# A two-branch kernel on one core: early products padded with zeros, loads and tables regrouped, and a new order of work

## The chip, the core and the metric

The kernel runs on one core of a Trainium2 chip. A core has a matrix engine (TensorE, PE in the profile; its weight loads are PEld), a vector engine (VectorE, DVE), a scalar engine (ScalarE, ACT), GpSimd (POOL) and SyncE (SP), which here only issues DMA transfers. Each engine works through its own queue in order and waits on semaphores for the others. The metric is the device time of one execution in microseconds; the kernel before has a median of 127.74 us over three runs (127.66 to 128.27).

## What is computed

Two independent branches whose outputs are put side by side, for 2048 tokens and width D = 448:

```python
# A: attention with 16 heads of 28, each token sees 8 tokens at distances 0, 2, ..., 14
qkv = x @ wqkv
logits = q . k[pos - off] * scale ; masked where pos - off < 0
attn = softmax(logits) ; o = attn . v ; a = o @ wo
# B: a diagonal complex state space of 448 states
Lam_bar = exp(exp(log_dt) * Lam) ; B_bar = (Lam_bar - 1) / Lam * Bmat
h[t] = Lam_bar * h[t-1] + B_bar x[t]
b = 2 * Re(C h) + x * Dskip
out = concatenate([a, b])
```

## The kernel before

All 2048 tokens are held in SBUF. The tokens of A are loaded in three parts: the first 512, the second 512 and the last 1024 (u = 0 is the first 1024, u = 1 the last). The first 1024 are transposed on TensorE (XI for the first 512, XA and XH for the second 512) and copied from PSUM into xT (xi, xa, xh); the last 1024 are transposed by DMA (L176). D = 448 is split into three blocks of 128 and one of 64: the block of 64 is kept for both halves s of 512 tokens at once, half 0 on partitions 0 to 63 and half 1 on partitions 64 to 127.

Queries and keys are made in seven column groups m (even m queries, odd m keys, m = 6 the rest of both, packed by wj): QK(u, m, k) is a step for both halves s. With k = 0 it runs the three blocks of 128 rows for both halves, with k = 1 the two products of 64 rows, one per half, on the two halves of the array. QS(m, s) (L349) is the same for one half, used at the start: three products of 128 rows (L354) and one of 64 (L355). Results go from PSUM to SBUF by qk and qh. V_ and v make the values in the same way.

P(u, r, ws) multiplies queries with four shifted views of the keys on VectorE (L385, 2048 wide) into one of seven buffers pr; E_(u, r) sums them per head with narrow products on TensorE (32 columns of the array; E_06 and E_16 also with 64 rows). lt, TD, sma, smb and smc make the softmax. AL, al, ad and sp lay the weights out as bands in the tile PT through DRAM; AV multiplies them with the values (32 columns of the array again), W_ with wo.

For B, PP transposes the raw parameters, and pcopy, pa, pb, pc, pd_, pe, pf and pg make the constants from them: pa is the exponential of log_dt on ScalarE, pc five further exponentials rk, pf sines, pg sixteen small operations on VectorE. The states stand in seven groups g of 64 complex ones. ty and tf make the angles of a group (ScalarE and VectorE, 256 wide), ts(0..2, g) the sine, the absolute value and the cosine on ScalarE. BD transposes B by DMA into BT, xt transposes the tokens of B into xbuf, where the tokens of A stood. BU multiplies the two (again k = 0 whole, k = 1 the halves of 64 rows). BR, z, UP and y carry four tokens together, sa, sb and sd are the scan of a pair of groups on VectorE, DN, dn, H_, h, hp, hy and hz bring the states back to all tokens, and C, c and oc give the output.

The order of all this is written out by hand in ORDER (L32). Each word is one step; the digits are its arguments, the digits after @ the PSUM banks it takes, and a final point or an equals sign puts a copy on ScalarE or on VectorE. Instructions enter each engine's queue in that order, and an engine never runs a later instruction before an earlier one. The loads at the start are issued by SP, the small parameters and one weight piece by ScalarE; a transfer waits for the one eight places before it.

Of the kernel before, what the change touches and what calls it, by code (L numbers as in the profile page):

```python
# [9 lines left out]
BF16 = mybir.dt.bfloat16  # L10
# [9 lines left out]
N2 = NC // 2  # L20
# [12 lines left out]
WU@0 XI0@1 xi00. xi01. XI1@2 XI2@3 xi10= xi11. PP@4 xi20= pcopy pa QS00@5 pb QS10@6 qk000. pd_ pc XH1@7 pe XA10@0 xh1=  # L33
XA11@1 qk010. xa10= QK021@32 xa11. QK031@45 P000 ty0 QS01@6 pf QS11@7 P001 QK051@01 QK030 tf0 qk011. qk001. pg ty5 tf5
ts00 ts10 qk030. ts20 QK020 qk020. ts05 QK041@76 P010 ty2 tf2 BD QK050 qk031. QK040 wj= QK061@43 ts15 qk050. ts02
qk051. qk021. P011 P020 P021 qk041. V_111@50 ts25 QK060 P030 ty1 qk040. V_000@12 E_00@67 E_01 qh001. P031 tf1 qh000.
P040 qh011. qh010. V_110 V_001 v000. ts12 P041 hc0 E_03 P050 P051 P060 v001. v110. E_02 V_010@43 v111. V_011 ts01 ts11
v010. ts22 ty6 tf6 QK110@12 QK111 QK100@50 QK101 P061 qk110. QK121@41 qk100. E_05 E_04 qk101. P100 P101 qk111. v011.
QK130@50 E_06 QK131 ts21 ty4 tf4 qk131. QK120 qk130. lt00 lt01 qk120. qk121. ts06 ts16 ts26 E_10@23 P110 QK150@30
QK151 ts04 ts14 qk151. QK141@56 QK161@74 P111 QK160 qh110. P120 P121 P130 ts24 qk150. QK140 qk141. qh111. V_100@10  # L40
V_101 v100. qk140. v101. P131 TD0 sma0 xt1 qh101. V_500@36 V_501 P140 v500. V_411@41 xt0 E_12 xt2 hc1 xt3 V_410 qh100.
LC V_400@50 V_401 v501. v410. v400. E_11 v411. E_13 V_510@76 smb0 P141 P150 P151 v401. E_14 V_511 ty3 P160 E_15
BU001@45 v511. BU101@10 P161 E_16 lt11 lt10 TD1 BU100 smc0 OZ v510. z10. BU200@63 BU000 LD ab ci2= CD2 ci0. CD0 rb0
ci3. CD3 z00. AL0@2 al0. ci1= AL1@7 al1. BR11 z11. BR01 BU010@14 z01. CD1 sma1 smb1 BU201 z20. tf3 BU011 BU301@27 BR02
BU111@05 z02. BU300 ts03 dk= BR03 rb3 smc1 BR21 ad1 z21. z30. z03. BU211@61 BU110 BR12 BU210 z12= BR13 BR22 BU401@32
xd0 ca3 ca6 ad0 cs3 z22. UP0 BR31 y0= xd3 xd1 OP pm3 BU400 wo AX@0 cs6 z13. z31. UP1 y1. ax. z40. sa0 ca1 BU310@46
BU500@75 BU501 BU311 z50= pm4 BR41 BR32 AL2@0 ca2 al2. z32. sb0 BU511@37 z41. BR23 z23= pm0 BR51 pm1 z51. sp0 AL3@0
BU510 BR33 ts13 al3. z33. BR52 BU411@42 z52. cs1 sp1 UP3 y3. UP2 y2. sd0 BU601@50 cs2 ts23 sa2 DN0@3 BR53 z53. BU410
ca4 BR42 DN1@6 dn1 BU600 z42. hp021 BR43 sb2 z60. dn0 UP5 AV020@1 AV031@6 sd2 AV000@4 z43. av031. cs4 UP4 y4. BU611@35
y5. av020. AV010@6 adx av010. AV030@2 AV021@7 BR61 BU610 sa4 z61. DN3@1 ad2 dn3 sb4 BR62 av021. AV001@6 av000. av030.  # L50
AV011@0 H_03@7 DN2@4 z62. BR63 dn2 ad3 H_00@2 W_20@1 z63= UP6 av011. H_01@3 h03 av001. W_01@0 ca5 ca0 W_11@6 w20= sd4
pm2 w01. w11. hp012 sp2 spx y6= h00 sa6 W_21@4 sp3 H_02@7 W_10@1 ow20 cs0 DN4@0 W_00@6 hp020 w10. w00. w21. W_31@5 h02
hp011 W_30@2 w30. sb6 DN5@1 AV111@6 AV110@4 av111. dn5 dn4 AV100@7 ow01 AV120@2 w31. av120. av110. ow11 AV121@1
AV131@6 cs5 sw2 ow10 av121. hp013 AV130@0 hp025 sw0 AV101@5 hp112 hp014 sd6 av100= C32@2 sw4 h01 hp023 DN6@4 dn6
av131= hp122 hp016 av130. hp022 hp120 hp010 C30@1 hp111 av101= H_05@7 h05 hp121 H_04@3 H_06@4 h04 h06 C33@6 C31@5
hp123 W_71@7 hp110 c30 oc30 xd2 hp113 sw6 ow30 ow31 hp125 hp115 c31 c32 oc32 c33 hy2 hy1 C00@3 W_60@4 c00 hz2 hy0 w71.
hz1 W_51@0 W_50@1 hp114 hy3 hp015 hz0 C02@5 C01@2 hz3 hp124 hp024 hp126 W_61@6 w61. hp026 hy5 hy4 oc31 ow71 ow00 C03@3
ow21 oc33 c01 oc01 hz5 hp116 W_40@7 hz4 hy6 W_41@6 w51. w50. W_70@2 ow51 hz6 C12@0 ow61 w41. w60. C11@1 c02 c03 C10@6
c10 c11 c12 w40. w70. C13@4 ow60 C20@5 C21@7 ow50 oc00 ow40 C22@3 CH0@2 c13 oc02 ow41 oc10 oc11 oc03 oc12 ow70 CH1@6
oc13 c20 c21 oc21 c22 oc20 oc22 ch0 oh0 ch1 oh1  # L60
# [3 lines left out]
def kernel(  # L64
# [109 lines left out]
    xT = s2.tile([128, 2, 7, 512], BF16, tag="xT")  # L174
# [15 lines left out]
    hpib, phi, sg, sscale = (cols[:, i:i + 1] for i in range(4))  # L190
    POOL.memset(hpib, 0.5 * PI * SHR)
    for col, lo, hi in ((phi, 0.0, 0.25), (sg, 2.0, -2.0), (sscale, 2 * PI * SHR, -2 * PI * SHR)):
        POOL.memset(col[0:64], lo)
        POOL.memset(col[64:128], hi)
# [85 lines left out]
    @op  # L280
    def XI(h):

        p = pp["xi", h] = ps(BF16)
        if h == 2:
            for t in range(4):
                PE.transpose(p[0:64, 128 * t:128 * t + 128], xnA[:, t, 384:448], ident[:])
            return
        for t in range(2):
            for f in range(3):
                PE.transpose(p[:, 256 * f + 128 * t:256 * f + 128 * t + 128], xnA[:, 2 * h + t, 128 * f:128 * f + 128], ident[:])  # L290

    @op
    def xi(h, k, e):
        p, c = pp["xi", h], 256 * h
        if h == 2:
            evict(e, xT[0:64, 0, 3], p[0:64, 0:512])
# [20 lines left out]
    @op  # L317
    def XH(b):
        p = pp["xh", b] = ps(BF16)
        for t in range(4):  # L320
            PE.transpose(p[64 * b:64 * b + 64, 128 * t:128 * t + 128], xnA[:, 4 * b + t, 384:448], ident[:])

    @op
    def xh(b, e):
        r = slice(64 * b, 64 * b + 64)
        evict(e, xT[r, 0, 3], pp.pop(("xh", b))[r, 0:512])
# [6 lines left out]
    def wqk(m, rows, kt):  # L333

        if m < 6:
# [13 lines left out]
    def QS(m, s):  # L349
# [5 lines left out]
        PE.matmul(p[:], wqk(m, slice(64 * s, 64 * s + 64), 3), xT[64 * s:64 * s + 64, 0, 3], start=False, stop=True)  # L355
# [243 lines left out]
    def pd_():  # L599
# [3 lines left out]
        V.tensor_scalar(fT[:], fT[:], -1.0, None, ALU.mult)  # L603
# [41 lines left out]

    @op
    def ty(g):
        pp["fr", g] = keep.tile([128, N2], F32, tag="fr", name="fr", bufs=2)
        ACT.activation(pp["fr", g][:], iot[:], ACTF.Identity, scale=fT[:, g:g + 1])

    @op
    def tf(g):

        kM, fr = keep.tile([128, N2], F32, tag="kM", name="kM")[:], pp["fr", g][:]
# [4 lines left out]
    def ts(i, g):  # L659

        fr = pp["fr", g][:]
        if i == 0:
            ACT.activation(tab[:, 1, g], fr, ACTF.Sin, scale=sscale)  # L663
        elif i == 1:
            ACT.activation(fr, fr, ACTF.Abs)
        else:
            ACT.activation(tab[:, 0, g], fr, ACTF.Sin, bias=hpib, scale=-2 * PI * SHR)
# [8 lines left out]
    @op  # L676
    def BD():
        SP.dma_start(BT.rearrange("p g b n -> p (g b) n"), Bn.rearrange("p g d -> p (g d)"), transpose=True)
# [305 lines left out]
```

## Time and profile before

| | |
|---|---|
| median of three runs | 127.74 us |
| the profiled execution, whole | 128.18 us |
| its span, first to last instruction | 126.5 us |
| mean granted TensorE clock | 1.000 |
| products on TensorE | 1045 |
| DMA | 22.33 MB in 57604 packets |

The page of the profile gives the busy time of each engine, the chain of work that ended last, and the costliest groups of instructions; further views give the timeline (start, duration, engine, line, operation, shapes, and in brackets the idle time just before and what ended it), the groups by line with the mean duration in ns, and the busy time of each engine in chosen stretches. In such a stretch the columns are the length, then PE, PEld, DVE, ACT and POOL busy with their instructions, the granted clock, the DMA share and GB/s. A merged row of the timeline, such as x3, runs from the first start to the last end. The numbers by which the change is judged are shown with the prediction.

### The profile page before, as it was taken

Reading aid. Unit: us, or ns where it says so; the run is one execution under the profiler, and the core shown is the slowest. Engines: PE = TensorE matmul, PEld = TensorE weight load, DVE = VectorE, ACT = ScalarE, POOL = GpSimd, SP = SyncE. Lnnn points to the kernel's source line nnn. Section 1 sums busy time; section 2 is a strip of 40 time slices with the busy share of each in tenths; the row PEclk is TensorE's granted clock in tenths of the full one; section 3 lists DMA queues with packets and bytes.
Section 4 is the critical chain, followed back from the end, with each engine's and each line's share of the span. In section 5 each row is a group of like instructions: output and inputs, shape, how many; then the busy total and the mean of one; then the engine's idle time right before and its main releaser. Section 6 shows DMA issues by size and latency. Waiting matters only on the chain.

```text
span 126.5 us, 2882 instructions
## 1 busy us (share of the span) xinstructions
PE 119.8 (95%) x1045; PEld 56.8 (45%) x1053; DVE 113.9 (90%) x220; ACT 105.2 (83%) x209; POOL 21.8 (17%) x40
## 2 busy tenths in 40 slices
PE   6989999999999999999999999999999999999990
PEld 6542334333334343463334444644585555555560
DVE  5769899999999999999999999999999999993850
ACT  0859999998899989898999999999999999991000
POOL 6800000000000002960199920000000000000000
PEclk9999999999999999999999999999999999999999
DMA  3896998999999998269899899899964242436442
GB/s 98 233 227 166 277 293 160 155 225 208 194 249 212 211 213 209 77 134 166 269 297 154 138 141 353 209 115 145 140 174 110 48 136 86 149 110 218 153 145 66
DMA packets 57604, 22.33 MB, mean 177 GB/s; under 512 B 44183, under 2 KB 57047, under 8 KB 57591
## 3 DMA queue, kind: packets, MB, share of 16 engines
q1 hardware_dynamic: 57384, 22.12, 79.7%
q8 instruction: 8, 0.13, 0.5%
q10 hardware_dynamic: 207, 0.04, 0.2%
q14 instruction: 5, 0.04, 0.1%
HBM read 9.86 MB, written 6.37 MB: 128 GB/s over the span
## 4 chain that ended last, share of the span: by engine, by line
DVE 40%; PE 33%; ACT 13%; DMA 6%; issue 4%; DVEq 0%; ACTq 0%
DVE pr L385 19%; PE ps L865 16%; PE ps L553 9%; DMA xbuf<-in_A_x_dram 4%; ACT Z L114 3%; ACT ctmp L690 2%; DVE fr L656 2%; PE ps L540 2%; DMA raw<-in_B_Lambda_re_dram 2%; DVE R L672 2%; DVE z L444 2%; PE ps L795 1%; PE ps L246 1%; ACT qf L114 1%; ACT kf L114 1%
## 5 line engine op out<-in xcount | busy, mean ns | idle before, releaser
L385 DVE TENSOR_TENSOR pr<-qf,kf 128x2048 bf16<-128x2048 bf16 x24 | 27.8, 1219 | 0.0
L246 PE MATMUL ps<-xbuf,BT 128*128 128x512 bf16 (+1 forms) x108 | 24.0, 380 | 0.5 <-issue 0.3
L865 PE MATMUL ps<-Cw,Z 128*128 128x448 bf16 x105 | 21.0, 353 | 0.0
L246 PE MATMUL ps<-xT,wq 128*128 128x512 bf16 (+1 forms) x94 | 20.5, 381 | 0.4 <-issue 0.2
L246 PEld LDWEIGHTS <-BT 128*128 128x128 bf16 (+1 forms) x112 | 9.0, 97 | 12.3 <-issue 3.7
L865 PEld LDWEIGHTS <-Z 128*128 128x128 bf16 x105 | 10.2, 98 | 9.5
L114 ACT CAST Z<-ps 128x512 bf16<-128x512 f32 (+1 forms) x29 | 13.7, 524 | 0.4 <-PE ps L741 0.2
L553 PE MATMUL ps<-wo,oT 128*128 128x448 bf16 x64 | 13.4, 352 | 0.0
L246 PEld LDWEIGHTS <-wq 128*128 128x128 bf16 (+1 forms) x96 | 7.2, 97 | 12.4 <-issue 4.7
L246 PE MATMUL ps<-wq,xT 128*128 128x448 bf16 (+1 forms) x64 | 12.6, 355 | 0.0
L941 POOL MEMSET PT<- 128x4320 f32 x3 | 11.0, 3696 | 5.5 <-ACT tab L663 5.5
L690 ACT ACTIVATE ctmp<-Cw,c2t 64x448 f32<-64x448 bf16 x14 | 9.3, 666 | 0.2
L553 PEld LDWEIGHTS <-oT 128*128 128x128 bf16 x64 | 6.2, 98 | 5.8
L114 ACT CAST v_s<-ps 128x448 bf16<-128x448 f32 x16 | 8.1, 531 | 0.5 <-PE ps L246 0.4
L246 PEld LDWEIGHTS <-xT 128*128 128x128 bf16 (+1 forms) x64 | 5.0, 97 | 7.8 <-issue 3.8
L114 ACT CAST ya<-ps 128x448 bf16<-128x448 f32 (+1 forms) x16 | 7.9, 548 | 0.6 <-DMA out_dram<-ya 0.6
L114 ACT CAST oT<-ps 128x512 bf16<-128x512 f32 x14 | 7.8, 628 | 0.1
L114 ACT CAST qf<-ps 128x512 bf16<-128x512 f32 x12 | 6.8, 595 | 1.4 <-PE ps L355 0.9
L917 POOL MEMSET Z<- 128x14 bf16 x1 | 0.1, 113 | 43.5 <-DMA Cr<-in_B_C_re_dram 43.5
L114 ACT CAST kf<-ps 128x512 bf16<-128x512 f32 x12 | 6.8, 576 | 0.5 <-PE ps L246 0.5
L729 PE MATMUL ps<-Z,R 128*128 128x512 bf16 x20 | 6.6, 381 | 0.2 <-DVE Z L114 0.2
L397 PE MATMUL ps<-pr,E 128*32 128x512 bf16 x96 | 6.7, 383 | 0.0
(168 smaller groups left out, 214.2 us busy)
## 6 DMA issues: line engine op xcount, KB each, us to landing
PT<-pd SPq DMA_DIRECT2D x16, 156.0 KB, 4.5
out_dram<-ya SPq DMA_DIRECT2D x16, 112.0 KB, 1.7
out_dram<-xbuf SPq DMA_DIRECT2D x15, 112.0 KB, 1.7
pd<-Ak SPq DMA_DIRECT2D x2, 640.0 KB, 3.3
xbuf<-in_A_x_dram SPq DMA_DIRECT2D x2, 448.0 KB
xnB<-in_B_x_dram SPq DMA_DIRECT2D x4, 224.0 KB
xnB<-in_B_x_dram SPq DMA_DIRECT2D x4, 192.0 KB, 4.6
PT<-Z SPq DMA_DIRECT2D x6, 128.0 KB, 3.5
```

Of the source, the lines that this page charges most:

```text
L114: (ACT.copy if e == "A" else V.tensor_copy)(o, i)
L246: PE.matmul(o, l, r, start=(first and i == 0), stop=(not first and i == len(pairs) - 1 and not more[s]))
L385: V.tensor_tensor(t[:], q.unsqueeze(1).to_broadcast((128, 4, 512)), k4, ALU.mult)
L397: PE.matmul(acc[s][32 * i:32 * i + 32], E[:, f, ws, :], t[:, i, :], start=(f == 0 and ws == 0), stop=False)
L444: V.reciprocal(z[:, :, 16:32], z[:, :, 0:16])
L540: PE.matmul(p[32 * hh:32 * hh + 32, 128 * bl:128 * bl + n], v_s[:, t, 4 * hg + hh, :], PT[:, t % NS, (4 * hg + hh) // HS, (4 * hg + hh) % ...
L553: PE.matmul(p[:, 0:D], late["oT"][:, b // 4, hg, par, 128 * (b % 4):128 * (b % 4) + 128], late["wo"][:, hg, :], start=(hg == 0), stop=(hg ...
L656: V.scalar_tensor_tensor(fr, kM, MAGIC, fr, ALU.subtract, ALU.subtract)
L690: ACT.activation(t[a:a + 64, 0:D], Cw[b:b + 64, g, :], ACTF.Copy, scale=c2t[a:a + 64, g:g + 1])
L729: PE.matmul(pp["z", g, j][:], rot(g, 0), late["Z"][:, g, j - 1, :], start=False, stop=True)
L865: PE.matmul(p[:, 0:D], z, Cw[:, g, :], start=(g == 0), stop=(g == G - 1))
L941: POOL.memset(late["PT"][:, 4 * i:4 * i + 4].rearrange("p t g n -> p (t g n)").bitcast(F32), 0.0)
```

## The change

Six things change at once.

1. The last products of QS become 128 rows high. A new tile wzz holds the 64 weight rows of half 0 with zeros under them, and those of half 1 with zeros above them; a memset puts zeros into the half of xT that is not yet filled. Three memsets on VectorE stand ahead of the ones for v_s and Ak. All eight QS (m = 0 to 3, s = 0 and 1) are used, where before m = 2 and 3 went through QK.
2. The transposes of the last 64 columns (XI2, XH) take 128 columns, of which the copy reads the upper half.
3. The weight columns 128 to 255 are loaded ahead of the second 512 tokens, and the first half's small piece is one transfer of 256 columns from ScalarE's queue instead of two of 128.
4. The sign of the sine for the lower 64 partitions goes into the angle (way instead of sscale), and the three steps ts run over two groups at once, 512 wide (the seventh group alone): 12 activations instead of 21.
5. The DMA transpose of B is issued in two parts, four groups and three.
6. ORDER is written anew, with other banks and other engines for some copies. xi00, xi01, two more al, three more w and three more y are on VectorE; xi10, the first xa, wj, dk, one more av and two more z on ScalarE.

```diff
 ORDER = """
-WU@0 XI0@1 xi00. xi01. XI1@2 XI2@3 xi10= xi11. PP@4 xi20= pcopy pa QS00@5 pb QS10@6 qk000. pd_ pc XH1@7 pe XA10@0 xh1=
-XA11@1 qk010. xa10= QK021@32 xa11. QK031@45 P000 ty0 QS01@6 pf QS11@7 P001 QK051@01 QK030 tf0 qk011. qk001. pg ty5 tf5
+WU@0 XI0@1 xi00= xi01= XI2@2 PP@3 pcopy pa XI1@4 xi10. xi20= pb pd_ pc pe xi11. QS00@5 QS10@6 QS30@7 XH1@0 ty0 ty1 pf
+tf0 tf1 XA10@1 xh1= QS20@3 pg ab rb0 ts00 xa10. XA11@2 xa11. QK050@40 qk000. xt0 qk010. P000 qk020. QS11@1 qk011. P001
+QS01@2 qk001. qk030. ts10 P010 ts20 ty4 QS21@5 QS31@6 qk031. qk021. QK041@31 tf4 QK051 P011 V_101@27 QK040 V_100 wj.
...
+    wzz = s2.tile([128, 2, 2, 256], BF16, tag="wzz")
+    for r in range(2):
+        V.memset(wzz[64 * r:64 * r + 64, 1 - r].rearrange("p a n -> p (a n)").bitcast(F32), 0.0)
+    xT = s2.tile([128, 2, 7, 512], BF16, tag="xT")
+    V.memset(xT[64:128, 0, 3], 0.0)
...
+        if c < 256 and len(at) == 2:
+            o = wzz[64 * s:64 * s + 64, s, :, c:c + n]
         eng.dma_start(o, i)
...
-    w_half(0, 0, 128, 0, D, eng=ACT)
+    w_half(0, 0, 256, 0, D, eng=ACT)
     SP.dma_start(xnA[:, 0:2], xA_r[:, 0:2])
     SP.dma_start(xnA[:, 2:4], xA_r[:, 2:4])
     w_load(0, 128, 0, D)
+    w_load(128, 128, 0, D)
     SP.dma_start(xnA[:, 4:8], xA_r[:, 4:8])
     w_half(1, 0, 256, 0, D)
-    w_load(128, 128, 0, D)
-    w_half(0, 128, 128, 0, D)
...
-            PE.transpose(p[64 * b:64 * b + 64, 128 * t:128 * t + 128], xnA[:, 4 * b + t, 384:448], ident[:])
+            PE.transpose(p[:, 128 * t:128 * t + 128], xnA[:, 4 * b + t, 320:448], ident[:])
...
-        PE.matmul(p[:], wqk(m, slice(64 * s, 64 * s + 64), 3), xT[64 * s:64 * s + 64, 0, 3], start=False, stop=True)
+        PE.matmul(p[:], wzz[:, s, m % 2, 64 * (m - m % 2):64 * (m - m % 2) + 128], xT[:, 0, 3], start=False, stop=True)
...
-        V.tensor_scalar(fT[:], fT[:], -1.0, None, ALU.mult)
+        V.tensor_scalar(fT[:], fT[:], way, None, ALU.mult)
...
-    def ts(i, g):
-
-        fr = pp["fr", g][:]
+    def ts(i, q):
+
+        fr, gs = pair(q, pp["fr", q]), slice(2 * q, 2 * q + 2 if q < 3 else G)
         if i == 0:
-            ACT.activation(tab[:, 1, g], fr, ACTF.Sin, scale=sscale)
+            ACT.activation(tab[:, 1, gs], fr, ACTF.Sin, scale=2 * PI * SHR)
...
-    def BD():
-        SP.dma_start(BT.rearrange("p g b n -> p (g b) n"), Bn.rearrange("p g d -> p (g d)"), transpose=True)
+    def BD(i):
+        gs = slice(4 * i, 4 + 3 * i)
+        SP.dma_start(BT[:, gs].rearrange("p g b n -> p (g b) n"), Bn[:, gs].rearrange("p g d -> p (g d)"), transpose=True)
```

In the rest of the new order, up to the first product of B (BU300, before it was BU001), the steps on which the timing of the start depends follow each other like this: QK060, V_000, V_011, QK061, V_001, E_00, E_02, E_01, V_010, V_400, QK110, E_03, QK100, QK120, E_04, E_05, E_06, lt00, lt01 on TensorE and ScalarE; on SP xt0, TD0, BD0, xt2, xt3, xt1, the loads of C, BD1, TD1. The first band product is AV021 (before AV020), and the last scan is followed by C32 and DN6 in both.

More of the change, by code (lines that the diff above doesn't have):

```diff
@@ L43 @@
[L43 to L47, printed above, removed]
@@ L189 @@
     cols = const.tile([128, 5], F32, tag="cols")
-    hpib, phi, sg, sscale = (cols[:, i:i + 1] for i in range(4))
+    hpib, phi, sg, way = (cols[:, i:i + 1] for i in range(4))
     POOL.memset(hpib, 0.5 * PI * SHR)
-    for col, lo, hi in ((phi, 0.0, 0.25), (sg, 2.0, -2.0), (sscale, 2 * PI * SHR, -2 * PI * SHR)):
+    for col, lo, hi in ((phi, 0.0, 0.25), (sg, 2.0, -2.0), (way, -1.0, 1.0)):
         POOL.memset(col[0:64], lo)
@@ L285, in XI @@
             for t in range(4):
-                PE.transpose(p[0:64, 128 * t:128 * t + 128], xnA[:, t, 384:448], ident[:])
+                PE.transpose(p[:, 128 * t:128 * t + 128], xnA[:, t, 320:448], ident[:])
             return
@@ L333, in wqk @@
     def wqk(m, rows, kt):
+        if m < 4 and kt == 3:
+            return wzz[rows, rows.start // 64, m % 2, 64 * (m - m % 2):64 * (m - m % 2) + 128]
         if m < 6:
@@ L644, with pair @@
     tab = keep.tile([128, 2, G, N2], BF16, tag="tab")
+    def pair(q, t):
+        return t[:, 0:2 if q < 3 else 1]
     @op
     def ty(g):
-        pp["fr", g] = keep.tile([128, N2], F32, tag="fr", name="fr", bufs=2)
-        ACT.activation(pp["fr", g][:], iot[:], ACTF.Identity, scale=fT[:, g:g + 1])
+        if ("fr", g // 2) not in pp:
+            pp["fr", g // 2] = keep.tile([128, 2, N2], F32, tag="fr", name="fr")
+        ACT.activation(pp["fr", g // 2][:, g % 2], iot[:], ACTF.Identity, scale=fT[:, g:g + 1])
     @op
     def tf(g):
-        kM, fr = keep.tile([128, N2], F32, tag="kM", name="kM")[:], pp["fr", g][:]
+        kM, fr = keep.tile([128, N2], F32, tag="kM", name="kM")[:], pp["fr", g // 2][:, g % 2]
         V.tensor_scalar(kM, iot[:], fT[:, g:g + 1], MAGIC, ALU.mult, ALU.add)
@@ L666, in ts @@
         else:
-            ACT.activation(tab[:, 0, g], fr, ACTF.Sin, bias=hpib, scale=-2 * PI * SHR)
+            ACT.activation(tab[:, 0, gs], fr, ACTF.Sin, bias=hpib, scale=-2 * PI * SHR)
     @op
```

52 lines of the change are left out of this document (27 added, 25 removed).

## The prediction

> **What bounds the kernel now.** I read the page first (busy shares, chain of waits), then the busy time by stretch, then TensorE's part of the timeline from 5 to 13 us.
>
> ```profile
> span 126.5 us, 2882 instructions
> PE 119.8 (95%) x1045; PEld 56.8 (45%) x1053; DVE 113.9 (90%) x220; ACT 105.2 (83%) x209; POOL 21.8 (17%) x40
> ...
> DVE 40%; PE 33%; ACT 13%; DMA 6%; issue 4%; DVEq 0%; ACTq 0%
> ```
> ```profile
> 13.00:95.00 82.00, 80.83 (x812) 35.78 (x818) 79.93 (x145) 78.14 (x157) 16.91 (x11) 1.00 0.97 197
> 95.00:123.10 28.10, 28.03 (x155) 14.94 (x153) 23.94 (x51) 19.15 (x35) 0.00 (x0) 1.00 0.43 128
> ```
>
> From 13 to 95 us TensorE is idle for 82.00 - 80.83 = 1.17 us, VectorE for 2.1, ScalarE for 3.9; from 95 to 123.1 us only TensorE is full. The chain runs through VectorE and ScalarE because they are full too, but the end is TensorE's queue run dry. So a change pays if TensorE has less to do or waits less, and if the other two keep up. The granted clock is 1.00 throughout.
>
> "Busy" hides one thing, which shows in single starts:
>
> ```profile
> 6.75 0.82 PE L354 MATMUL ps<-xT,wq 128*128 128x512 bf16 x3
> 7.50 0.39 PE L355 MATMUL ps<-xT,wq 64*128 64x512 bf16 x1
> 8.39 0.41 PE L321 MATMUL ps<-ident,xbuf 128*64 128x128 bf16 x4 [0.50 <-DMA xbuf<-in_A_x_dram]
> 8.73 0.84 PE L307 MATMUL ps<-ident,xbuf 128*128 128x128 bf16 x12
> 9.64 0.60 PE L246 MATMUL ps<-xT,wq 64*128 64x512 bf16 x4
> 10.18 0.82 PE L354 MATMUL ps<-xT,wq 128*128 128x512 bf16 x2
> 10.93 0.39 PE L355 MATMUL ps<-xT,wq 64*128 64x512 bf16 x1
> 11.25 0.82 PE L354 MATMUL ps<-xT,wq 128*128 128x512 bf16 x3
> ...
> 12.54 2.27 PEld L246 LDWEIGHTS <-wq 128*128 128x128 bf16 x12 [0.42 <-issue]
> ```
>
> Three whole products of 512 columns last 0.82 and one lasts 0.39, so a start follows a start after (0.82 - 0.39)/2 = 0.215: a slot. From the half product at 10.93 to the next whole one at 11.25 it is 0.32; from 6.75 to the half product at 7.50 it is 0.75, not 0.645. Every change of the tile's shape, in or out, costs 0.10 to 0.11 us in which nothing runs.
>
> **The change part by part.** *Shapes.* Shapes are 128x128, half rows (64x128), 32 columns (E_, AV), E_06 and E_16 (64x32), 64-column transposes, and PP (7 rows). Going through both order lists, the shape changes 76 times before, 56 after. The eight half products of QS and the 64-column transposes become whole, and the later halves of QK, V_ and BU stand next to each other more often. At 0.10: -2.0 us (-1.6 to -2.2).
>
> *Padded halves.* For m = 0 to 3 of the first 1024 tokens there were 4 x 4 slots (QS) and, for m = 2 and 3, 12 whole products and 4 halves that run two at a time: 30 slots. Now 8 x 4 = 32: +0.43 us. TensorE's own sum: -1.5 us. [...]
>
> *The way to 13 us.* The new order puts new work in front of the first products, so I walk it with these rows (the first is the chain of waits).
>
> ```profile
> 2.91 5.44 DMA xbuf<-in_A_x_dram
> ```
> ```profile
> 1.05 0.48 DVE L227 MEMSET v_s<- 128x512 uint32 x1
> 2.02 2.19 DVE L229 MEMSET Ak<- 128x2560 f32 x1 [0.48 <-issue]
> 4.13 0.13 DVE L233 TENSOR_TENSOR Is<-ident 128x64 bf16<-128x64 bf16 x1
> ...
> 4.83 0.76 DVE L114 COPY xT<-ps 128x512 bf16<-128x512 bf16 x2 [0.58 <-PE ps L290]
> 5.52 0.16 DVE L582 CAST P<-ps 128x21 f32<-128x21 bf16 x1
> 5.71 0.21 ACT L586 ACTIVATE dt<-P 128x7 f32<-128x7 f32 x1
> 5.96 0.43 DVE L590 TENSOR_TENSOR are<-dt,P 128x7 f32<-128x7 f32 x1 [0.28 <-ACT dt L586]
> ...
> 7.33 0.60 ACT L596 ACTIVATE rk<-are 128x7 f32<-128x7 f32 x5
> ...
> 9.62 0.58 ACT L114 COPY xT<-ps 128x512 bf16<-128x512 bf16 x1 [1.10 <-PE ps L307]
> 10.00 2.35 DVE L385 TENSOR_TENSOR pr<-qf,kf 128x2048 bf16<-128x2048 bf16 x2
> 10.10 0.51 ACT L649 ACTIVATE fr<-iot,fT 128x256 f32<-128x256 f32 x1
> 10.62 1.28 ACT L615 ACT_TABLE_LOAD   x1
> ...
> 12.54 0.56 ACT L114 CAST kf<-ps 128x512 bf16<-128x512 f32 x1
> 13.00 0.59 ACT L114 CAST qf<-ps 128x512 bf16<-128x512 f32 x1
> ```
> ```profile
> L663 ACT ACTIVATE tab<-fr,cols 128x256 bf16<-128x256 f32 x7 | 3.6, 513 | 0.1
> ...
> L114 ACT COPY xT<-ps 128x256 bf16<-128x256 bf16 x2 | 0.7, 376 | 0.0
> ```
>
> Three memsets of 256 words are new on VectorE: v_s and Ak give (2.19 - 0.48)/2048 = 0.83 ns a word, so 0.27 each, 0.8 together, of which 0.48 may fall into the hole before Ak. Is then ends at 4.6 to 5.1. Three copies follow (0.34, 0.22, 0.16): the constants are out at 5.3 to 5.8. On ScalarE the exponential (0.21) now stands ahead of xi10 (0.58): 6.1 to 6.6. Then rk (0.60), released by VectorE's "are" after xi20, and xi11 (0.38) behind it: 7.1 to 7.6. That is what QS00's third product waits for. Two slots, then QS10 and QS30 with four each: 9.2 to 9.7.
>
> There XH1 needs the second 512 tokens, which landed at 2.91 + 5.44 = 8.35. Now two weight loads go out ahead of them; bounds are 8.35 (the loads run beside them anyway) and 10.6 (issued 1.3 later, and 192 KB at the 226 GB/s of the row below). I take 9.3, the issue alone: no wait.
>
> ```profile
> 5.00:10.00 5.00, 4.11 (x34) 1.79 (x31) 3.78 (x18) 2.92 (x12) 1.30 (x4) 1.00 0.91 226
> ```
>
> ScalarE meanwhile has two ramps (0.41 apart), the table load (1.28), three small ones (0.64) and the first sine of two groups. A copy of 512 takes 0.21 more than one of 256, so that sine takes 0.51 + 0.21 = 0.72: 10.5 to 11.1. Behind it stand xa10 (1024 wide, 0.58 + 0.42 = 1.0), xa11, and two evictions at 0.46: xa10 is there at 11.5 to 12.1, VectorE's first product P000 starts at 13.0 to 13.5, not at 10.00. TensorE waits for xa10 before QK050's second product and ends QK050 at 12.7 to 13.3; I take 13.0.
>
> At 13.0 the old kernel has run 16 slots of QS, 2 pairs at 9.64, one pair at 12, and 2 of the products begun at 12.54: 21. The new one has 22, of a total that is 2 larger, so one slot more is left (+0.2), but 54 shape changes against 62 (-0.8). From 13 us on TensorE has 0.6 us less: **-0.6** (-0.9 to -0.3 by the dates; +0.7 with the tokens at 10.6).
>
> *VectorE.* By 13 us it has done the pg block, two tf and rb0, which came later before: some 4.6 us more ahead of P000, while up to the last scan it gets 1.8 more (al, y and w evictions come over, xa10, wj and two z leave). So 2.8 less is left, and P000 is 3.0 to 3.5 later: 0.2 to 0.7 late at the last scan.
>
> ```profile
> 95.37 0.29 DVE L777 TENSOR_TENSOR Z<-vv,p 128x256 bf16<-128x256 bf16 x1
> ...
> 96.17 0.27 PE L782 MATMUL ps<-Z,R 128*128 128x256 bf16 x1
> ```
>
> That scan ends at 95.66, and its first user, behind which all products of the end queue, starts at 96.17: cover 0.5. I cost it at nothing, at most +0.2.
>
> *ScalarE.* Three pairs of groups take 2.1 instead of 2.9 us per pair by durations (+0.21 on each of three): up to -2.4, less by starts. The evictions moved cancel within 0.1 us. Against the 1.17 us of middle waits I take -0.1 (0 to -1.0).
>
> [...]
>
> *B's transpose in two.*
> ```profile
> 31.17 5.25 SPq L678 DMA_TRANSPOSE BT<-Bn  x1
> ...
> 37.86 8.07 SPq L702 DMA_TRANSPOSE xbuf<-xnB  x4
> ```
> One xbuf transpose (2.0) now runs where BT stood, behind it the band transpose and 16/28 of BT (3.0), then the other three: done at about 45, as before (45.9). Its first user BU300 comes at about 48.6. Nothing, with 2 us of cover; the second part is wanted 10 us later.
>
> The sum: 128.18 (the profiled execution) - 0.6 - 0.1 = 127.5. That execution lies 0.44 above the median of 127.74, so the median becomes **127.0**. I call 0.5% (0.64 us, below 127.10 or above 128.38) what a measurement can tell from no change.
>
> **The rivals.** *A: the order also removes middle waits.* For it: ScalarE's 2 us of relief and 0.1 us steps in the waits; against: VectorE gains work. All 1.17 us: 127.0 - 1.0 = 126.0.
>
> *B: shortened TensorE is only given back as waits.* VectorE is 97% busy from 13 to 95 us and gets 1.1 us more in all, and padding without its saving costs 0.43. Then the shapes' -2.0 shrinks to what the early waits took: 127.6.
>
> *C, slower: P000 comes late.* Place: ScalarE's line ts00, xa10, xa11, qk000, qk010. It decides once P000 starts after 13.3 (2.8 + 0.5 behind 10.00): from there each microsecond delays last scan and end alike. With tokens at 10.6, XH1 and XA10 (0.9) give xa10 a start at 11.5 and P000 at 14.1; with its seven pr buffers full, P031 waits 0.7 more for E_00. That is 1.5 past the point: 127.0 + 1.5 = 128.5. Against it: the loads ahead share 16 queues with the tokens.
>
> **How the numbers follow.** Forecast 0.40 (126.6 to 127.5), A 0.17, B 0.19, C 0.24. Below 127.10: A and two thirds of the forecast less a little, 0.17 + 0.30 + some of B's low end = 0.50; above 128.38: most of C, 0.24; the rest 0.26. The range takes in A's end and C with a further 0.3: 125.9 to 128.8.
>
> **What would show it.** Right: no 64-row product at L362, two changes of shape before 13 us, third product of QS00 at 7.1 to 7.6, QK050 over at 13.0, P000 at 13.0 to 13.5, TensorE idle about 1.1 us from 13 to 95. Wrong: tokens landing after 10, P000 after 14, a stall of TensorE before BU300, AV021 or DN6, or VectorE idle by more than 3 us from 13 to 95.

## The result and the profile after

The changed kernel takes 129.80 us (median of 20 executions, 128.22 to 131.85); the kernel before, on the same chip, 127.87 (20 executions, 127.60 to 128.42). The ratio is 1.0104, 95% interval 1.0076 to 1.0131: slower by 1%. Its executions spread over 3.6 us, those of before over 0.8. The profile is of the longest one (131.85 us, in whose records the clock is lower in places); what is read from it here is held against a second profiled execution, of 129.96 us, in the first experiment.

The page of the changed kernel: span, busy shares, the granted clock by slices, and the chain of waits.

```profile
span 130.1 us, 2878 instructions
PE 120.3 (92%) x1043; PEld 58.5 (45%) x1053; DVE 118.4 (91%) x225; ACT 102.7 (79%) x198; POOL 20.1 (15%) x40
...
PEclk9977999999999999999999999999999999999999
...
PE 53%; DVE 22%; SPq 5%; DMA 5%; issue 5%; POOLq 3%; POOL 3%; ACT 2%; DVEq 0%
```

Two things are new against before: slices three and four of the clock, and GpSimd with 6% of the chain (POOL and POOLq), where it had none. The page of the second execution has neither: all its clock slices are 9, and its chain is PE 69% and DVE 26%, without GpSimd. The busy time by stretch (us, then TensorE, weight loads, VectorE, ScalarE, GpSimd, granted clock), and the last stretch of the second execution behind it:

```profile
5.00:10.00 5.00, 3.26 (x14) 1.43 (x13) 4.47 (x23) 4.03 (x14) 1.29 (x4) 0.79 0.97 236
10.00:15.00 5.00, 5.00 (x33) 2.64 (x32) 3.13 (x20) 3.60 (x7) 1.03 (x4) 0.87 0.98 268
```
```profile
13.00:95.00 82.00, 78.49 (x658) 34.36 (x665) 80.29 (x128) 73.81 (x143) 14.63 (x9) 1.00 1.00 189
```
```profile
13.00:95.00 82.00, 80.78 (x767) 35.72 (x765) 80.23 (x132) 75.53 (x147) 14.77 (x9) 1.00 1.00 194
```

From 13 to 95 us TensorE waits 82.00 - 78.49 = 3.5 us in the first execution, but only 1.22 in the second, against 1.17 before. So idle time of TensorE behind 13 us is not what the kernel loses. TensorE's timeline at the start, and then VectorE's and GpSimd's at two later places, say more.

```profile
4.77 0.51 PE L296 MATMUL ps<-ident,xbuf 128*128 128x128 bf16 x6
6.64 0.59 PE L361 MATMUL ps<-xT,wq 128*128 128x512 bf16 x2 [1.36 <-ACT xT L114]
7.39 0.38 PE L361 MATMUL ps<-xT,wq 128*128 128x512 bf16 x1 [0.16 <-ACT xT L114]
...
8.99 0.63 PE L362 MATMUL ps<-xT,wzz 128*128 128x512 bf16 x1
...
10.70 0.63 PE L362 MATMUL ps<-xT,wzz 128*128 128x512 bf16 x1
11.12 0.50 PE L327 MATMUL ps<-ident,xbuf 128*128 128x128 bf16 x4
...
12.99 0.38 PE L252 MATMUL ps<-xT,wq 128*128 128x512 bf16 x1
```

The last transposes of the first tokens are followed by 1.36 us without work. Then a product of 512 columns lasts 0.38, but at 8.99 and 10.70 it lasts 0.63: there a start follows a start after 0.427 us, twice a slot. QK050 begins at 12.99, where the prediction had it end.

```profile
15.45 2.35 DVE L392 TENSOR_TENSOR pr<-qf,kf 128x2048 bf16<-128x2048 bf16 x2
...
48.54 2.35 DVE L392 TENSOR_TENSOR pr<-qh_t,kh 128x2048 bf16<-128x2048 bf16 x2
...
55.98 3.13 DVE L665 TENSOR_SCALAR kM<-iot,fT 128x256 f32<-128x256 f32 x1
...
75.49 0.36 DVE L665 TENSOR_SCALAR kM<-iot,fT 128x256 f32<-128x256 f32 x1
...
100.91 0.29 DVE L788 TENSOR_TENSOR Z<-vv,p 128x256 bf16<-128x256 bf16 x1
```
Two such rows of the kernel before, the last pair of products and one such step:
```profile
48.76 2.35 DVE L385 TENSOR_TENSOR pr<-qh_t,kh 128x2048 bf16<-128x2048 bf16 x2
...
58.39 0.35 DVE L655 TENSOR_SCALAR kM<-iot,fT 128x256 f32<-128x256 f32 x1
```
GpSimd after the change:
```profile
55.90 0.85 POOL L950 MEMSET wo<- 128x896 f32 x1
56.68 1.17 POOL L948 MEMSET oT<- 128x1280 f32 x1
57.79 1.17 POOL L948 MEMSET ya<- 128x1280 f32 x1
64.72 10.98 POOL L952 MEMSET PT<- 128x4320 f32 x3 [5.75 <-DMA Cw<-Cn]
```

P000 starts at 15.45. The last pair of products of VectorE (P160 and P161, the row with qh_t) starts at 48.54; before the change it was 48.76, so by then nothing is lost. The step tf2 then takes 3.13 us for an instruction that took 0.35, from just behind the start of GpSimd's memsets to 0.15 us behind their end (57.79 + 1.17 = 58.96). The last scan ends at 101.20 (99.32 in the second execution); before it was 95.66. Not all of this is lost: in the new order ten products of 448 or 512 columns that stood behind the last scan stand ahead of it (150 and 140 products start behind it in the run of before without xd0 and xd1 and in the run with filler), and the span ends 28.9 us behind the scan in both executions, where it ended 30.8 behind. For the second execution that makes 3.66 - 1.90 = 1.76 us, the difference of the two spans (128.22 and 126.46). So the date of the last scan carries the loss; between 50 us and the scan it shows, although its first cause may lie earlier.

### The profile page after: what moved, and what is told of

Read it like the earlier page. It is cut to its first block, busy times and chain, and to the rows that moved or that the text cites. A ratio compares the mean times of both kernels' runs of the same rounds, so it can differ in the third digit from the quotient of the medians.

```text
span 130.1 us, 2878 instructions
## 1 busy us (share of the span) xinstructions
PE 120.3 (92%) x1043; PEld 58.5 (45%) x1053; DVE 118.4 (91%) x225; ACT 102.7 (79%) x198; POOL 20.1 (15%) x40
## 4 chain that ended last, share of the span: by engine, by line
PE 53%; DVE 22%; SPq 5%; DMA 5%; issue 5%; POOLq 3%; POOL 3%; ACT 2%; DVEq 0%
PE ps L876 15%; PE ps L252 11%; DVE pr L392 10%; PE ps L560 9%; PE ps L361 5%; SPq L516 4%; PE ps L547 4%; POOL PT L952 3%; POOLq L990 3%; DMA pdx<-Ak 3%; DVE kM L665 2%; DMA Cw<-Cn 2%; DVE Ak L235 2%; PE ps L362 2%; PE ps L404 2%
## 5 line engine op out<-in xcount | busy, mean ns | idle before, releaser
L252 PE MATMUL ps<-xbuf,BT 128*128 128x512 bf16 (+1 forms) x109 | 25.1, 380 | 0.6 <-ACT Z L114 0.3
L252 PE MATMUL ps<-xT,wq 128*128 128x512 bf16 (+1 forms) x69 | 15.4, 379 | 0.4 <-issue 0.3
L252 PEld LDWEIGHTS <-wq 128*128 128x128 bf16 (+1 forms) x72 | 5.9, 97 | 8.4 <-issue 2.5
L361 PE MATMUL ps<-xT,wq 128*128 128x512 bf16 x23 | 7.5, 429 | 1.7 <-ACT xT L114 1.5
```

Source lines behind the costliest of these rows:

```text
L252: PE.matmul(o, l, r, start=(first and i == 0), stop=(not first and i == len(pairs) - 1 and not more[s]))
L361: PE.matmul(p[:], wqk(m, slice(0, 128), kt), xT[:, 0, 4 * s + kt], start=(kt == 0), stop=False)
```

## The experiments

The line numbers of a kernel with an added function are some lines higher: L671 or L670 is L665 of the changed kernel. Each time is a median, followed by its ratio to the kernel before on the same chip.

**1. The changed kernel again, and TensorE kept busy.** The first run changes nothing; the second adds products of zeros that nobody reads.

```diff
+    def WF():
+        p = ps()
+        for _ in range(24):
+            PE.matmul(p[:, 0:128], wz[:], wz[:], start=True, stop=True)
-... XI1@4 xi10. xi20= ...
+... XI1@4 WF@0 xi10. xi20= ...
```

> The changed kernel once more, unchanged, to see which of its features come back. Theory: two things cost it time. One is an accident of the start: TensorE idles 1.53 us from 5.06 to 6.64, after which its products start every 0.427 us instead of 0.215 from 8.14 to 11.12; where that comes back P000 starts at 15.4, where it does not, at about 13.4, and the time differs by up to 2 us. The other belongs to the order: the angle instruction of VectorE at L665 that takes 3.13 us at 55.98 instead of 0.35, beside GpSimd's memsets from 55.81 to 58.96; it comes back in every execution, within 1 us of 3.1. Rival: the new order of the middle is slow by itself, then both differ from execution to execution and the time stays at 129 to 130. Time expected: 129.8 (128.2 to 131.9).

> 24 products of zeros (128 columns, 0.053 us each, 1.3 us together) are put between the last transposes of the first 512 tokens and QS00, in the stretch 5.06 to 6.64 in which TensorE idled; nothing reads them. Theory (the idle stretch is what halves the clock at 8.14): starts every 0.215 us throughout, QS00's third product at 7.4 as before, QK050 over at 13.2 or earlier, P000 at 13.5, and the time no longer has the upper half of its spread: median 128.9 (128.2 to 129.5). Rival (the clock falls for another reason, or the late P000 is made good later by slack of VectorE): the median stays at 129.8.

Measured: unchanged 129.77 (1.0104, interval 1.0064 to 1.0144), with filler 128.27 (1.0029, 1.0015 to 1.0044), and its 12 executions lie within 0.6 us. TensorE's timeline of the unchanged kernel, and its clock by stretch:

```profile
4.95 0.82 PE L296 MATMUL ps<-ident,xbuf 128*128 128x128 bf16 x6
6.64 1.44 PE L361 MATMUL ps<-xT,wq 128*128 128x512 bf16 x3 [0.87 <-ACT xT L114]
...
8.30 1.48 PE L361 MATMUL ps<-xT,wq 128*128 128x512 bf16 x3
...
10.97 0.38 PE L362 MATMUL ps<-xT,wzz 128*128 128x512 bf16 x1
```
```profile
5.00:10.00 5.00, 4.13 (x15) 1.74 (x15) 4.47 (x23) 4.03 (x14) 1.29 (x4) 1.00 1.04 235
```

and of the kernel with filler, TensorE and then VectorE:

```profile
5.49 2.15 PE L277 MATMUL ps<-wz 128*128 128x128 bf16 x24
7.48 0.81 PE L367 MATMUL ps<-xT,wq 128*128 128x512 bf16 x3
...
11.83 1.46 PE L252 MATMUL ps<-xT,wq 128*128 128x512 bf16 x6
13.12 0.81 PE L367 MATMUL ps<-xT,wq 128*128 128x512 bf16 x3
```
```profile
14.29 3.49 DVE L398 TENSOR_TENSOR pr<-qf,kf 128x2048 bf16<-128x2048 bf16 x3
```

Three products last 1.48 without filler and 0.81 with it. The slow stretch also comes where the granted clock is given as 1.00 (5 to 10 us of the unchanged kernel): it is to be read from the starts, not from that column. It came at different dates in the two unchanged executions (8.1 to 11.1, and 6.6 to 10.4), and not in this one with filler.

What followed the idle stretch was not the same in both. The traces of before and of the changed kernel begin at half speed: their first 22 products, of 128 columns, start 0.107 us apart (from 1.06 to 3.3 us), later ones 0.056 apart. In the first execution the change comes at 4.83 us, ahead of the gap (six products in 0.51), and the half speed returns behind it, at 8.14. In the second it has not come when the transposes end (six products in 0.82), and half speed goes on behind the gap, up to 10.4. With filler the change comes at 6.8 us, within the filler products, and full speed stays (QS00 to QK050, three products in 0.81). So full speed ended behind the gap once and came only behind it once. The length of the gap alone does not decide: in the run with Ak's memset early on GpSimd (experiment 5) a gap of 1.56 us, from 10.79 to 12.36, is followed by starts every 0.215 us.

With filler QK050 (the row at 11.83) is over when the next product starts at 13.12, the last pair of P starts at 47.38, and P000 at 14.29, not 13.5: VectorE still has pg and rb0 ahead of it. Filling the idle stretch gained 1.5 us of the median.

**2. The step beside the memsets moved (tf2), alone and with filler.**

```diff
-... smc0 OZ ... rb3 tf2 BU200 ...
+... smc0 tf2 OZ ... rb3 BU200 ...
```

> The step tf2 (two VectorE instructions, 0.77 us) is moved from behind rb3 to directly behind smc0, ahead of OZ, so that it runs before GpSimd's memsets begin. Theory (VectorE is kept out by GpSimd's memsets for 2.8 us, and all that follows it is late by that): L665 takes 0.35 us, TensorE's waits of 1.0 us at 62.1 and 1.1 us at 68.2 go, and the time falls by 1.5 to 2.5 us: 127.8 (127.3 to 128.3). Rival (VectorE has slack there, TensorE waits for ScalarE's copies): below 0.5 us of gain, 129.5.

> Filler products and tf2 moved, together. Theory: both gains add, since one lies in the start and one at 56 us: 127.0 (126.5 to 127.5), below the kernel before. Rival (they hide each other, since a late P000 and a late VectorE are the same lateness): no better than the better of the two alone, 127.8 or more.

Measured: 129.66 (1.0104, 1.0061 to 1.0148) and 128.78 (1.0049, 1.0028 to 1.0070). The instruction took 0.35 us in the first, as expected, and the time stayed. The theory that this one step carries the loss was wrong; where the gain went was open until experiment 6. Together with filler it is no better than filler alone (128.27): there tf2 still met the memsets, which had come earlier too, and took 0.62 us.

**3. What an added or a missing piece of VectorE's work costs.** The kernel before with one more memset of Ak ahead of P000; the kernel with filler without xd0 and xd1; the kernel before without them.

> The kernel before with one more memset of Ak on VectorE (2.19 us by its row) put directly ahead of its first product P000, which then starts at about 12.2 instead of 10.00; nothing else. It measures what a late P000 costs where nothing else is new. Theory (VectorE is full from P000 to the last scan, and the end follows the last scan): scan end 2.19 less the cover of 0.5 later, time +1.7: 129.6 (129.2 to 130.1). Rival, as the prediction had it (TensorE sets the end, and a P000 earlier than 13.3 costs nothing): 128.0 (127.9 to 128.3).

> The kernel with the 24 filler products, without the steps xd0 and xd1: B's input isn't multiplied by D for half of the tokens; that is 2.0 us of VectorE between 63 and 69 us and nothing else. It measures what VectorE's time ahead of the last scan is worth. Theory (VectorE sets the last scan, and the end follows it by 25.2): scan end 1.7 to 2.0 earlier, 126.4 (126.1 to 126.9). Rival (the waits of TensorE from 64 us on come from ScalarE or from the transfers of PT): 128.0 or more.

> The kernel before, without its steps xd0 and xd1: B's input isn't multiplied by D for half of the tokens. It asks what bounded the kernel before. Theory now (VectorE, through the last scan): 126.3 (126.0 to 126.8). As the prediction had it (TensorE's queue, with 1.17 us of waits from 13 to 95 and a cover of 0.5 at the last scan): 127.6 (127.3 to 128.0).

Measured: 131.85 (1.0258, 1.0209 to 1.0306), 128.25 (1.0035, 1.0023 to 1.0048) and 128.03 (1.0002, 0.9988 to 1.0016). The first says less than hoped: P000 came at 14.2, the profiled execution had a granted clock of 0.987 as the longest one of the changed kernel had, and the copy wj, late in VectorE's queue, let TensorE wait 2.76 us. The other two are plain misses of the theory: 2.0 us less of VectorE changed neither kernel's time. For the kernel before that means that VectorE wasn't its bound at this place, as the prediction had said. For the new one it pointed to something else that sets a date behind it.

**4. Padding away, padding alone, the parts in the old order.** The last product of QS over its 64 rows again (with filler); padding put into the kernel before; all parts of the change under the old order, twice (the second time with the old order of loads and with tables moved behind wj).

```diff
-        PE.matmul(p[:], wzz[:, s, m % 2, ...], xT[:, 0, 3], start=False, stop=True)
+        PE.matmul(p[:], wqk(m, slice(64 * s, 64 * s + 64), 3), xT[64 * s:64 * s + 64, 0, 3], start=False, stop=True)
```

> With the filler products, but the last product of each QS again over its 64 rows alone, as before the change; the zeros are still made. It takes the padding away and leaves the order. Each of the eight half products brings two changes of shape at 0.10 us. Theory (each change of shape costs TensorE 0.10 us, and TensorE is full up to 64 us): 1.6 us of TensorE more by 17 us, P000 0.3 to 0.6 later, 129.2 (128.7 to 129.9). Rival (the changes of shape are hidden, VectorE alone decides): 128.5 or less.

> The kernel before with the padding alone: zeros beside the half weights, QS00, QS10, QS01 and QS11 and the transposes of the last columns over the whole array; its order, its loads' order (the half weights of columns 128 to 255 come with the first), its tables and its transpose of B stay. Twelve changes of shape fewer, of which those before 8.4 us are hidden by the wait for the second 512 tokens; three memsets more (0.8 us) at the start of VectorE. Theory (a change of shape costs 0.10 us up to UP1): -0.4, 127.6 (127.2 to 128.0). Rival (the memsets push the start, or VectorE decides): 128.0 to 128.6.

> The parts of the change without its order: the changed kernel's code (padded half products in QS00, QS10, QS01 and QS11, angle tables per two groups, B's transpose in two issues one behind the other, its order of loads) under the order list of before; tables of groups (0,1), (4,5), (2,3), 6 stand where those of 0 and 5, 2 and 1, and so on stood. Theory (the new order loses the time, by the late P000 and by work of VectorE ahead of the last scan): P000 at 10 to 11 and the time no worse than before, 127.5 (126.7 to 128.1). Rival (one of the parts costs the time): 128.6 or more.

> The parts of the change in the order of before, now also with the loads in the order of before (the second 512 tokens ahead of the second weights) and with the tables of groups 4 and 5 behind wj, so that VectorE doesn't wait with wj behind it (1.93 us in the run before). Padded are QS00, QS10, QS01 and QS11; tables per two groups; B's transpose in two. Theory (the order loses the time, not the parts): P000 at 10.0 to 10.3, no wait of TensorE over 0.7 us after 13, and 127.6 (126.9 to 128.1). Rival (a part costs the time): 128.6 or more.

Measured: 129.62 (1.0127, 1.0097 to 1.0157), 128.01 (1.0010, 0.9981 to 1.0039), 131.76 (1.0264, 1.0213 to 1.0315) and 130.72 (1.0227, 1.0184 to 1.0271). By the records the shape changes 70 times in the first, against 56 with filler: fourteen more, not sixteen, since the last half product of QS31 now stands beside those of QK041. They cost 129.62 - 128.27 = 1.35 us, 0.096 each (1.25 and 0.090 by the ratios, as the two were measured beside different executions of the kernel before). Padding alone makes the changes 8 fewer (68 instead of 76), not twelve, and gave no gain that the median shows. TensorE's first rotation UP0 comes at 65.36 instead of 65.77, the 0.4 expected, but P000 is as much earlier (9.60 instead of 10.00): from P000 to UP0 nothing is gained, and the trace doesn't show that the 0.4 comes from the shapes. The two mixed orders tell nothing of the parts: VectorE and ScalarE waited there for each other's share of the tables (VectorE 1.9 and 2.2 us in one piece, TensorE behind it), and products ran at half speed (six of 512 columns in 2.74 us at 21.76 in the first, three in 1.46 at 20.94 in the second; granted clock 0.987 in both). Whether the paired tables pay in the old order stays open.

**5. Ak's memset on GpSimd, early and late.** With 24 filler products it stands at the end of GpSimd's opening work; with 16 behind the steps pg and ab.

> With the filler products, and the memset of Ak (2.19 us) on GpSimd behind its opening work instead of on VectorE ahead of Is. Theory (the date of P000 sets the last scan, and its chain begins with this memset): first copies of the first tokens about 0.9 earlier, P000 at 13.4, last scan 0.9 earlier: 127.4 (127.0 to 127.9). Rival (up to 64 us TensorE is the bound, which has no wait to lose there): 128.2.

> 16 filler products instead of 24, and the memset of Ak (2.19 us on VectorE, ahead of Is) moved to GpSimd behind the steps pg and ab, at about 14 us, where no VectorE instruction of the kind that waited in the run before (L613 and L614, 2.27 us beside this memset) stands within 2 us. Theory (date of P000 sets the last scan, which sets the end): QS00 at 6.2 to 6.8, P000 at 13.2 to 13.6 instead of 14.29, last scan at 97.0 to 97.4 instead of 98.0, time 127.5 (127.0 to 128.0). Rival (TensorE, without a wait from 5.7 to 64 us in the kernel with filler alone, is the bound): 128.2.

Measured: 129.91 (1.0155, 1.0116 to 1.0195) and 127.93 (1.0016, 0.9996 to 1.0036). The early place shows, unasked, what the memsets do to VectorE. VectorE's and GpSimd's timeline there:

```profile
6.06 2.48 DVE L613 TENSOR_SCALAR fT<-f 128x7 f32<-128x7 f32 x1
6.27 2.27 DVE L614 TENSOR_SCALAR km<-f 128x7 f32<-128x7 f32 x1
8.58 0.17 DVE L615 SCALAR_TENSOR_TENSOR fT<-km,fT 128x7 f32<-128x7 f32 x1
```
```profile
6.28 2.23 POOL L235 MEMSET Ak<- 128x2560 f32 x1
```

An operation on seven elements, 0.16 us in the other kernels, lasts as long as the memset (2.27 beside 2.23). The late place gained 0.3 over the filler alone, not the 0.8 expected. In its trace tf2 met the next memsets (1.37 us instead of 0.35); that trace is of the longest execution (128.73 us), so that this is shown for it and not for the median.

**6. Who pins the last scan.** A last step taken out of the stretch ahead of it (xd2, moved behind it), alone and with the other causes mended:

> The kernel with 24 filler products, xd2 (1.0 us of VectorE) moved from between y1 and cs6 to behind h06, after the last scan; nothing else. Theory (between UP1 and the last scan VectorE is the bound, and there alone): last scan 1.0 earlier, 97.0, and the time 127.3 (127.0 to 127.6). Rival (as with xd0 and xd1, the stretch waits for something else): 128.2.

> The changed kernel with all four causes mended: 16 filler products, Ak's memset on GpSimd at about 14 us, tf2 ahead of smc0 (before GpSimd's memsets), and xd2 behind h06, after the last scan. Theory (the causes lie one behind the other and add up): no wait of TensorE over 0.7 us but the one at 78 us, last scan at 96.3 to 96.8, time 126.8 (126.4 to 127.3), faster than the kernel before by 0.7 to 1.2%. Rival (xd2 is only handed on to the products of the end): 127.6.

Measured: 129.16 (1.0101, 1.0072 to 1.0130) and 128.75 (1.0066, 1.0042 to 1.0091): again the theory missed. The last scan of the first came no earlier than in the run without xd0 and xd1 (97.61 and 97.63), and xd2 got in the way later (TensorE waited 0.73 us for VectorE at 114.3). But its trace shows the pin. VectorE and GpSimd, without xd2:

```profile
70.30 1.98 DVE L671 TENSOR_SCALAR kM<-iot,fT 128x256 f32<-128x256 f32 x1
...
97.32 0.29 DVE L794 TENSOR_TENSOR Z<-vv,p 128x256 bf16<-128x256 bf16 x1
```
```profile
61.16 10.98 POOL L958 MEMSET PT<- 128x4320 f32 x3 [5.03 <-DVE z L455]
```

and without xd0 and xd1:

```profile
71.21 1.09 DVE L671 TENSOR_SCALAR kM<-iot,fT 128x256 f32<-128x256 f32 x1
...
97.34 0.29 DVE L794 TENSOR_TENSOR Z<-vv,p 128x256 bf16<-128x256 bf16 x1
```
```profile
61.17 10.98 POOL L958 MEMSET PT<- 128x4320 f32 x3 [5.05 <-PE ps L252]
```

VectorE comes to tf6 at 70.30 or at 71.21, and is let through at the same date, 72.28 and 72.30, 0.14 us behind the end of the memsets of PT (61.16 + 10.98 = 72.14). Time saved ahead of tf6 is waited away at tf6. The dates of the changed order, all from such rows:

| kernel | end of PT's memsets | tf6's first instruction over | last scan over | scan behind memsets |
|---|---|---|---|---|
| changed, first profile | 75.70 | 75.85 | 101.20 | 25.50 |
| changed, again | 73.83 | 73.98 | 99.32 | 25.49 |
| tf2 moved | 73.64 | 73.78 | 99.12 | 25.48 |
| filler | 72.51 | 72.65 | 97.99 | 25.48 |
| filler, without xd0, xd1 | 72.15 | 72.30 | 97.63 | 25.48 |
| filler, xd2 moved | 72.14 | 72.28 | 97.61 | 25.47 |

Two limits of this table. Each row is one execution: the filler row is of 128.61 us, the next one of 128.24, and P000 differs already (14.29 and 13.88), so the 0.36 us between the two scans are not the work of xd0 and xd1. And a constant distance alone shows no hold: in six traces of the old order it is 22.0 to 22.1 us, although no such step is held there. What shows the hold is the length of the instruction, up to 1.98 us. In the changed kernel itself it is 0.36:

```profile
73.62 0.36 DVE L665 TENSOR_SCALAR kM<-iot,fT 128x256 f32<-128x256 f32 x1
```

There VectorE came to tf6 only 0.21 us ahead of the memsets' end, and tf6 cost nothing; it is what the time saved by the other steps runs into.

So tf6 itself was moved, alone, and then with the causes of the other experiments mended (16 filler products, Ak late on GpSimd, tf2 ahead of smc0):

```diff
-... sb0 AL3@6 tf6 BR41 ... sd0 y2= ca2 ...
+... sb0 AL3@6 BR41 ... sd0 y2= tf6 ca2 ...
```

> The kernel with 24 filler products, tf6 moved from ahead of sd0 to behind y2; nothing else. Theory: the 0.5 to 0.6 us for which tf6 is held by GpSimd's memsets of PT go, last scan at 97.4 instead of 98.0, no longer 25.5 behind the memsets' end, time 127.7 (127.5 to 128.0). Rival (VectorE isn't held by the memset, it is late by its own work): 128.3.

> 16 filler products, Ak's memset on GpSimd at about 14 us, tf2 ahead of smc0, and tf6 moved from ahead of sd0 to behind y2, so that it comes after GpSimd's memsets of PT; xd2 stays where the change put it. Theory (tf6 was held until these memsets ended; without it VectorE runs on): L671's instruction takes 0.35 us, last scan at 96.7 instead of 97.33 to 98.26, end 25.2 behind it, time 127.2 (126.9 to 127.6), faster than the kernel before by 0.3 to 0.8%. Rival (the transfers of PT, which wait for the same memsets, set TensorE's products of AV and through them the end): 127.9 as with e9_pool_late.

Measured: 127.66 (0.9976, 0.9957 to 0.9995) and 127.36 (0.9941, 0.9913 to 0.9969), both as the theory had it. In the first the last scan is over at 97.26 (the row below), 0.73 earlier than in the filler's trace and 24.9 behind the memsets, while VectorE has the same work ahead of it; that leaves the hold at tf6 as the cause.

```profile
96.97 0.29 DVE L794 TENSOR_TENSOR Z<-vv,p 128x256 bf16<-128x256 bf16 x1
```

Of the second, VectorE's timeline and the stretch from 13 to 95 us:

```profile
13.56 3.49 DVE L397 TENSOR_TENSOR pr<-qf,kf 128x2048 bf16<-128x2048 bf16 x3
...
47.04 2.36 DVE L397 TENSOR_TENSOR pr<-qh_t,kh 128x2048 bf16<-128x2048 bf16 x2
...
73.34 0.34 DVE L670 TENSOR_SCALAR kM<-iot,fT 128x256 f32<-128x256 f32 x1
...
96.55 0.29 DVE L797 TENSOR_TENSOR Z<-vv,p 128x256 bf16<-128x256 bf16 x1
```
```profile
13.00:95.00 82.00, 81.44 (x823) 36.22 (x822) 80.08 (x128) 76.14 (x147) 15.09 (x8) 1.00 1.03 197
```

TensorE waits 0.56 us from 13 to 95, half of what it waited before the change, and the kernel is faster than the one before by 0.6%.

**7. Evictions handed back.** From the end of sd0 to the end of sd6 it is 23.0 us in the new order and 20.0 in the old one, with VectorE busy for 22.5 and 19.5. By durations 1.8 us of the 3 are evictions that came over from ScalarE and 1.3 two steps, an h and a cs, that now lie inside the stretch. Three evictions (av010, av001, w30) went back, in the best version:

> As e16_best2, with the evictions av010, av001 and w30 on ScalarE again instead of VectorE (3 x 0.61 us of VectorE less between sd0 and sd6, about 1.6 us of ScalarE more). Theory (VectorE alone is the bound from UP1 to the last scan): last scan at 95.1 instead of 96.8, of which 0.6 to 1.0 is lost again because TensorE's tail has more left: 126.6 (126.2 to 127.0). Rival (ScalarE, 4.9 of 5 us busy there, becomes the bound): 127.3 to 127.8.

Measured: 132.23 (1.0320, 1.0269 to 1.0371), a miss on the rival's side and far beyond its number. Of TensorE's waits from 90 to 100 us there remains one:

```profile
PE ps L565 <- ACT ya L114: 2.3, 1, 2.3
```

The copy w30, now in ScalarE's queue behind others, holds the PSUM bank 3 that W_61 needs. The last scan came at 97.25, not at 95.1: VectorE was busy for less (21.7 us instead of 23.2 between sd0 and sd6) and still no earlier, so the theory that it alone is the bound there fell too. This trace is of an execution of 130.84 us; what the others lose beyond it isn't shown. In this order these three can't go back together; whether av010 and av001 can without w30 wasn't tried.

## Why the prediction was wrong

It said 127.0; the median is 129.8, outside its range. Two steps failed: the speed of the products at the start, and the durations of VectorE's steps between the last pair of P and the last scan. Point by point:

- *Changes of shape and padding on TensorE (-2.0 and +0.43).* The count was right (76 and 56 by the records, 62 and 54 of them from 13 us on), and a change cost 0.096 by the experiment. As a term of the time it was not: with filler QK050 ends at 13.1, as predicted, and UP0 comes at 63.66 instead of 65.77, but from there to TensorE's last product it is 59.80 us instead of 57.26. By single starts of the filler run and of the kernel before without xd0 and xd1, these 2.5 us are, as an estimate, 1.4 of waits, 0.6 of band products (5.41 instead of 4.82 us, in six runs instead of four), 0.3 of changes of shape and 0.2 of one product that stood ahead of UP0. So the kernel with filler is 0.3% slower where -0.6 us was forecast.
- *The way to 13 us.* Here the first step failed: "Two slots, then QS10 and QS30 with four each: 9.2 to 9.7". QS00's third product came at 7.39, within the dates of the walk; but the walk itself left TensorE idle for over a microsecond, and products behind that ran at 0.427 us, not 0.215. They ended 1.4 us after the dates given. The second 512 tokens were there in time, although 8.35 + 1.3 is 9.65 and not the 9.3 that was taken: with filler XH1 starts at 10.07 without a wait. P000 still came 0.8 late with filler (14.29): the walk followed ScalarE's line, and counted pg and rb0 as done by 13 us without walking their dates; on VectorE they stand from 10.96 to 14.29.
- *VectorE costs nothing, cover 0.5 at the last scan.* The second step that failed. Up to the last pair of P VectorE lost nothing (the pair starts at 48.49 in the second profile, 48.76 before, though P000 is 5.4 later), and from there to the last scan it took 50.83 us instead of 46.90 (tf2, tf6 and evictions came, rb0 and dk left). About 1 us of these 3.9 is one instruction: tf2 had moved into GpSimd's memsets, so that the duration of the old row (0.35) didn't hold; it took 3.13 and 1.30 us in the two profiles of the changed kernel. tf6 had moved there as well; it cost nothing while VectorE was late, and up to 1.6 us once the time ahead of it was saved. The prediction names no date of GpSimd.
- *ScalarE (-0.1) and B's transpose in two (nothing).* ScalarE's spare time grew, as the busy time from 13 to 95 us shows (75.5 in the second execution against 78.1), but where evictions wait it had none, as the last experiment shows. TensorE didn't wait at BU300.
- *Rival C, slower through a late P000.* Its sign was right, its point of decision (13.3) wrong: a P000 at 15.4 was made good by 48.5 us. What is right of it is that inside the new order a date is handed on: from the unchanged to the filler kernel P000, PT's memsets and the last scan come 1.11, 1.33 and 1.33 earlier. Rival A falls. Rival B's time (127.6) wasn't measured either, but its mechanism, a shorter TensorE given back as waits, is there with filler: 2.1 us earlier at UP0 and no gain at the end.
- *What would show it.* Of the signs of being right, TensorE's idle time from 13 to 95 us held (1.22), as did the two changes of shape and QS00's third product, and the time was wrong all the same: the idle time says nothing of products at half speed or of a later scan. Of the signs of being wrong, P000 after 14 happened. A change of speed, or a wait that lengthens an instruction instead of standing ahead of it, wasn't named. (In the chances, two thirds of 0.40 are 0.27, not 0.30; nothing hangs on it.)

From 129.77 to the best version the medians fall by 1.50 with filler, by 0.61 with tf6 moved and by 0.30 with tf2, Ak and fewer filler products, to 127.36, 0.4 above the forecast. The single shares depend on the order in which they are mended, since tf2 alone gained nothing. What is left open is what sets the start of PT's memsets: the profile names another releaser in nearly every execution.

## What to carry to other kernels

When a step is moved, look at what runs beside it on the other engines, not only at what stands ahead of it: here the 0.35 us read from a row of tf2's instruction became 3.13 beside GpSimd's memsets. When a walk of the start leaves TensorE idle, price the products behind the gap at both speeds that these traces show (a start every 0.215 or every 0.427 us), or fill the gap with products of nothing, which was worth 1.5 us here. And when work taken away brings nothing, look for a date that doesn't move in any of the traces, and then test it by moving the step: here a table of ends pointed to the pin after three theories had missed it, and the move showed it.

## What the hardware showed that was not expected

Behind a wait of 1.36 us in the first profile and of 0.87 in the second, both up to 6.64 us, TensorE ran at half speed (a start every 0.427 us instead of 0.215): from 8.1 to about 11.1 and from 6.6 to about 10.4 us. The granted clock from 5 to 10 us is given as 0.79 in the first and as 1.00 in the second. In the first TensorE had run at full speed ahead of the gap (six transposes in 0.51 us), in the second not yet (0.82). What sets the speed, and when it changes, these traces don't show; the gap of 1.56 us in experiment 5 was followed by full speed.

VectorE's operations on one f32 tensor with scalars (TENSOR_SCALAR) that met GpSimd's memsets lasted until a memset had ended, and it shows as a longer instruction, not as idle time: 2.27 us beside 2.23 (L614, 0.16 elsewhere), 3.13 instead of 0.35 across memsets that ended 0.15 earlier. The operation of the next line on two tensors kept its 0.43 us (with filler, at 55.37, beside ya's memset from 55.28 to 56.45). GpSimd's memset was longer in its turn: in the second execution ya's, begun at 57.02, took 1.31 us instead of 1.17, while tf2 ran on until 57.23. Why the two engines hold each other up isn't shown.
